# Projecting Q, K and V of a recurrent attention segment on four column groups of the TensorEngine, with V placed by DMA

## The chip, the cores and the metric

The kernel runs on one core of a Trainium2 chip. The metric is the device time of one launch in microseconds (us); smaller is better. Timed runs of a kernel and of the kernel before alternate on the same chip. The engines are named as in the profile: PE is TensorE (PEld its weight loads), DVE is VectorE, ACT is ScalarE, POOL is GpSimd, SP is SyncE, which here only issues DMAs.

## The reference, cut to what matters

The program is one training step (outputs and all gradients) of a block with a recurrent memory and a feed-forward layer, for 2048 tokens of 448 features. The tokens are cut into 64 segments of 32. Each segment is attended together with 8 memory rows, and the memory rows that come out are the input of the next segment. So 64 segments form a chain, forward, and another, backward.

```python
for s in range(n_seg):                        # 64 segments
    xs = x[:, s * seg_len:(s + 1) * seg_len, :]          # 32 rows of layernorm(x)
    h = jnp.concatenate([mem, xs], axis=1)               # 8 + 32 = 40 rows
    q = jnp.einsum('btd,dhe->bhte', h, Wq)               # 16 heads of 256
    k = jnp.einsum('btd,dhe->bhte', h, Wk)
    v = jnp.einsum('btd,dhe->bhte', h, Wv)
    scores = jnp.einsum('bhqe,bhke->bhqk', q, k) * scale
    p = _softmax(jnp.where(mask[None, None], scores, -1e9), axis=-1)
    o = jnp.einsum('bhqk,bhke->bhqe', p, v)
    o = jnp.einsum('bhte,hed->btd', o, Wo)
    mem = o[:, :M, :]                                    # 8 rows, to the next segment
    outs.append(o[:, M:, :])
# then h = x + outs, h2 = h + FFN(layernorm(h)); gradients of all of it by vjp
```

Everything but the memory rows is known from the start. Only `mem` is handed on, and it passes through every step above.

## The kernel before: the parts that matter

The kernel has four stages: the forward chain, the feed-forward stage, the backward chain, and a tail that computes the weight gradients.

In the forward chain, Q and K come out *feature-major* (features on the partitions): 32 blocks of 128 features, each with the 40 tokens as the moving operand. V comes out token-major on two column groups of 64.

```python
def wpass(W_sb, s, dst):                       # Q and K: 128 matmuls of 40 columns each
    ...
    for j in range(MC):                        # 32 blocks of 128 features
        for kc in range(KC):                   # 4
            nc.tensor.matmul(pss[b][:, jj * L:(jj + 1) * L], lhsT=W_sb[:, kc, c * P:(c + 1) * P],
                             rhs=hT_roll[:, kc, sl, :], ...)
# in the loop over segments, in the order in which they are written:
wpass(Wq_sb, s, qT)
wpass(Wk_sb, s, kT)
...                                            # scores, 32 short matmuls
for b in range(4):                             # V: 32 matmuls of 64 x 512
    for kc in range(KC):
        for g in range(2):
            nc.tensor.matmul(pV[b][64 * g:64 * g + 64, 0:512], lhsT=hT_flat[:, kc, sl * L:sl * L + 64],
                             rhs=Wv_sb[:, kc, n * 512:(n + 1) * 512], ...)
...                                            # softmax, evacuate V, transpose P
...                                            # P times V (16 matmuls); split off the 8 memory rows as o8
for j in range(MC):                            # memory rows times Wo
    nc.tensor.matmul(pO[32 * (j % 4):32 * (j % 4) + M, 0:D], lhsT=o8[:, j, :], rhs=Wo_sb[:, cj(j), :], ...)
...                                            # fp32 transposition of the sum of four groups -> hT_roll of s + 1
nc.gpsimd.dma_start(out=dr["QT"][s], in_=qT.rearrange("p c n -> p (c n)"))
nc.sync.dma_start(out=dr["KT"][s], in_=kT.rearrange("p c n -> p (c n)"))
```

The 32 x rows of four segments go through Wo together, as a full block of 128 rows, off the chain. The backward chain needs Q and K token-major, so it loads them with DMA transposes, and the tail reads whole tiles of attention rows from DRAM:

```python
def load_seg(s):                               # backward chain
    nc.sync.dma_start_transpose(out=vT..., in_=dr["VG"][s])
    nc.sync.dma_start_transpose(out=Q_sb, in_=dr["QT"][s])
    nc.sync.dma_start_transpose(out=K_sb, in_=dr["KT"][s])
...
src = dr["X_" + nm][t][:, hf * 2048:(hf + 1) * 2048]     # tail: one DMA, 128 partitions outermost
if nm == "o":
    nc.sync.dma_start(out=x_t, in_=src)
```

## Time and profile before

The kernel before took 3456.91 us (median of 3 runs, 3451.01 to 3477.07). The stages, read from the first and last instructions of each in the trace:

| stage of the kernel before | us |
|---|---|
| start to the first memory rows written for segment 1 | 82.5 |
| 62 more segments, 17.37 each on average | 1076.7 |
| end of the chain to the first feed-forward matmul | 84.2 |
| feed-forward | 322.7 |
| to the start of the backward chain | 44.8 |
| backward chain to the start of the tail | 1138.2 |
| tail | 712.6 |

The period of a segment is the time between two copies of the memory rows into the activations of the next segment (DVE, line 449).

One segment of the forward chain in the timeline of PE (columns: start, duration, engine, line, operation, operands, count; in brackets the idle time before it and what ended it):

```profile
604.24 6.55 PE L360 MATMUL psf<-arA,arW 128*128 128x40 bf16 x256 [0.28 <-DVE arA L449]
611.53 3.62 PE L399 MATMUL psf<-arW,arA 128*64 128x512 bf16 x30
615.16 0.38 PE L420 MATMUL psf<-ident,arB 128*40 128x40 bf16 x16
616.62 0.73 PE L428 MATMUL psf<-arB,arA 128*128 128x80 bf16 x16 [1.08 <-ACT arB L77]
617.42 1.69 PE L437 MATMUL po<-arW,arB 128*8 128x448 bf16 x32
```

Q and K (line 360) take 6.55 us, V (399) 3.62; the softmax runs under V; then P is transposed (420), P·V (428) waits 1.08 us for the evacuated P, and the memory rows go through Wo (437). Two stretches of the trace (window; length; busy time of each engine with its instruction count; clock; DMA share; GB/s), one in the forward chain and one in the backward chain:

```profile
300.00:600.00 300.00, 283.25 (x6902) 218.91 (x6899) 129.73 (x295) 96.38 (x211) 46.05 (x106) 0.99 0.45 141
1700.00:2200.00 500.00, 465.01 (x10749) 328.80 (x10753) 230.14 (x584) 187.33 (x485) 105.44 (x239) 0.98 0.78 166
```

PE is busy for 94% of the forward stretch. The DMA engines are busy for 45% there, and for 78% in the backward chain. What PE waited for in the forward chain from 80 to 1160 us (columns: what waited, what ended the wait; us in total, times, longest):

```profile
PE psf L428 <- ACT arB L77: 34.7, 32, 1.1
PE psf L446 <- DVE om L442: 9.0, 18, 0.6
```

There is little to wait for. So the forward chain is bound by PE's work.

### The profile page before, as it was taken

The numbers are of one execution on the slowest core, as the hardware profiler recorded it, in microseconds if no ns is written. First come the engines' busy times: TensorE is split into PE (matmuls) and PEld (weight loads), VectorE is DVE, ScalarE is ACT, GpSimd is POOL, SyncE is SP. The second block draws the span as 40 slices with busy tenths as digits, with TensorE's granted clock in tenths as the row PEclk, the third lists the DMA queues.
The fourth block names the chain that finished last, engine by engine and source line by source line (L and its number), as shares of the span: only waits on it lengthen the run. The fifth ranks groups of instructions, "written<-read, shape, count | busy, mean of one in ns | idle before, by whom it ended". The sixth has DMA issues, their size and how long they took to land.

```text
span 3461.7 us, 120955 instructions
## 1 busy us (share of the span) xinstructions
PE 3042.7 (88%) x55028; PEld 2056.9 (59%) x55038; DVE 1321.4 (38%) x2921; ACT 974.9 (28%) x2181; POOL 620.8 (18%) x1304
## 2 busy tenths in 40 slices
PE   3999999999999658892999999989999898999999
PEld 2777777777777446661666666666666544444444
DVE  4444444444444246771444444444444301111111
ACT  1333333333333223330333333333333202111100
POOL 3111111111111111111112211211221211111121
PEclk8999999999999879996999999999999999999999
DMA  7344633543534797799687878787887988888661
GB/s 264 132 130 133 174 127 130 162 146 127 156 130 147 134 210 182 178 212 239 139 164 167 174 161 165 166 160 163 172 167 162 275 241 185 174 176 179 160 247 38
DMA packets 997173, 583.91 MB, mean 169 GB/s; under 512 B 906100, under 2 KB 916420, under 8 KB 995060
## 3 DMA queue, kind: packets, MB, share of 16 engines
q1 hardware_dynamic: 926788, 340.27, 47.5%
q0 software_dynamic: 67568, 233.95, 19.8%
q8 instruction: 430, 7.05, 0.9%
q10 hardware_dynamic: 2304, 1.97, 0.2%
q14 instruction: 83, 0.68, 0.1%
HBM read 104.05 MB, written 250.19 MB: 102 GB/s over the span
## 4 chain that ended last, share of the span: by engine, by line
PE 61%; issue 13%; DMA 9%; DVE 8%; SPq 4%; ACT 2%; POOL 2%; ACTq 0%; DVEq 0%; POOLq 0%
PE psf L360 12%; PE po L756 8%; PE psf L399 6%; PE psf L713 5%; PE psf L691 4%; PE po L437 3%; PE fx L462 3%; PE fx L815 3%; PE psf L536 2%; PE psf L921 2%; PE psf L942 2%; PE psf L778 2%; DVE arA L75 2%; PE psf L446 2%; PE fx L602 2%
## 5 line engine op out<-in xcount | busy, mean ns | idle before, releaser
L77 ACT CAST arA<-psf 128x320 bf16<-128x320 f32 (+4 forms) x1139 | 487.9, 447 | 1595.2 <-PE psf L360 422.0
L75 DVE CAST arA<-psf 128x384 bf16<-128x384 f32 (+6 forms) x1029 | 492.5, 496 | 1075.9 <-PE psf L921 359.9
L360 PE MATMUL psf<-arA,arW 128*128 128x40 bf16 x16384 | 433.6, 181 | 62.0 <-POOL arA L345 35.8
L360 PEld LDWEIGHTS <-arW 128*128 128x128 bf16 x16384 | 432.2, 97 | 76.5 <-issue 57.3
L756 PE MATMUL po<-arW,arA 128*32 128x448 bf16 x6144 | 359.2, 365 | 40.5 <-DVE arA L75 21.0
L713 PE MATMUL psf<-arA,arW 128*128 128x40 bf16 x8192 | 219.2, 180 | 55.5 <-POOL arA L648 44.8
L921 PE MATMUL psf<-arW,arA 128*128 128x512 bf16 x990 | 250.7, 381 | 10.3 <-DMA arW<-X_k 5.3
L713 PEld LDWEIGHTS <-arW 128*128 128x128 bf16 x8192 | 214.9, 96 | 75.2 <-issue 74.8
L399 PE MATMUL psf<-arW,arA 128*64 128x512 bf16 x2048 | 259.5, 382 | 0.0
L756 PEld LDWEIGHTS <-arA 128*32 128x32 bf16 x6144 | 156.3, 98 | 160.7 <-issue 32.9
L536 PE MATMUL psf<-arA,arW 128*128 128x256 bf16 x1344 | 163.8, 283 | 94.4 <-DMA arA<-arA 68.7
L921 PEld LDWEIGHTS <-arA 128*128 128x128 bf16 x1440 | 135.2, 98 | 184.7 <-issue 39.2
L536 PEld LDWEIGHTS <-arW 128*128 128x128 bf16 x1344 | 136.3, 102 | 124.3 <-issue 100.4
L399 PEld LDWEIGHTS <-arA 128*64 128x64 bf16 x2048 | 147.3, 111 | 66.5 <-issue 0.2
L75 DVE CAST arB<-psf 40x320 bf16<-40x320 f32 x320 | 108.0, 337 | 98.1 <-PE psf L428 64.7
L77 ACT CAST arB<-psf 128x96 bf16<-128x96 f32 (+1 forms) x320 | 98.3, 307 | 103.5 <-DVE arB L75 51.0
L691 PEld LDWEIGHTS <-arW 128*128 128x128 bf16 x2048 | 88.4, 101 | 65.7 <-issue 62.1
L723 ACT COPY arA<-psf 128x1024 bf16<-128x1024 bf16 x128 | 123.3, 1015 | 4.7 <-PE psf L722 3.1
L462 PE MATMUL fx<-arW,arA 128*128 128x448 bf16 x512 | 124.5, 353 | 0.0
L437 PE MATMUL po<-arW,arB 128*8 128x448 bf16 x2048 | 110.7, 359 | 3.7
L691 PE MATMUL psf<-arB,arW 128*128 128x80 bf16 x2048 | 99.1, 203 | 16.7 <-DVE arB L740 7.7
L942 PE MATMUL psf<-arW 128*128 128x448 bf16 x450 | 95.4, 361 | 5.4 <-DMA arW<-X_o 5.3
(461 smaller groups left out, 3760.6 us busy)
## 6 DMA issues: line engine op xcount, KB each, us to landing
QT<-arA POOLq DMA_DIRECT2D x64, 512.0 KB, 4.0
KT<-arA SPq DMA_DIRECT2D x64, 512.0 KB, 3.5
VG<-arA SPq DMA_DIRECT2D x64, 512.0 KB, 3.1
X_o<-arA POOLq DMA_DIRECT2D x40, 512.0 KB, 4.5
X_v<-arA POOLq DMA_DIRECT2D x32, 512.0 KB, 6.2
X_k<-arA POOLq DMA_DIRECT2D x32, 512.0 KB, 4.2
X_q<-arA POOLq DMA_DIRECT2D x32, 512.0 KB, 4.2
arW<-X_o SPq DMA_DIRECT2D x30, 512.0 KB, 13.9
```

Source lines behind the costliest of these rows:

```text
L75: nc.vector.tensor_copy(out=out, in_=in_)
L77: nc.scalar.copy(out=out, in_=in_)
L360: nc.tensor.matmul(pss[b][:, jj * L:(jj + 1) * L], lhsT=W_sb[:, kc, c * P:(c + 1) * P], rhs=hT_roll[:, kc, sl, :], start=(kc == 0), stop=( ...
L399: nc.tensor.matmul(pV[b][64 * g:64 * g + 64, 0:512], lhsT=hT_flat[:, kc, sl * L:sl * L + 64], rhs=Wv_sb[:, kc, n * 512:(n + 1) * 512], sta ...
L437: nc.tensor.matmul(pO[32 * (j % 4):32 * (j % 4) + M, 0:D], lhsT=o8[:, j, :], rhs=Wo_sb[:, cj(j), :], start=(j < 4), stop=(j >= MC - 4), sk ...
L462: nc.tensor.matmul(px[:, 0:D], lhsT=xblk[:, j, :], rhs=Wo_sb[:, cj(j), :], start=(j == 0), stop=(j == MC - 1))
L536: nc.tensor.matmul(ps[:, f2 * 256:(f2 + 1) * 256], lhsT=Wt[:, kc, c * P:(c + 1) * P], rhs=xT[:, kc, :], start=(kc == 0), stop=(kc == KC - 1))
L691: nc.tensor.matmul(ps[b][:, i * 2 * L:(i + 1) * 2 * L], lhsT=lhs[:, cl, :], rhs=rhs_bd[:, cl // 2, :, :].rearrange("p g n -> p (g n)"), st ...
L713: nc.tensor.matmul(pss[b][:, jj * L:(jj + 1) * L], lhsT=WoT_sb[:, kc, c * P:(c + 1) * P], rhs=do_roll[:, kc, sl, :], start=(kc == 0), stop ...
L756: nc.tensor.matmul(pH[32 * (j % 4):32 * (j % 4) + 32, 0:D], lhsT=blk[nm][:, j, r * SEG:(r + 1) * SEG], rhs=WT[:, cj(j), :], start=(nm == " ...
L921: nc.tensor.matmul(pa[2 * kc + g][:, 0:w], lhsT=lhs_of(b)[:, kc * P:(kc + 1) * P], rhs=rhs_of(b, g), start=(b == 0), stop=(b == nblk - 1), ...
L942: nc.tensor.matmul(pa[i][:, 0:D], lhsT=lhs_of(b, i), rhs=rhs_of(b), start=(bi == 0), stop=(bi == len(nblk) - 1))
```

## The change

The intent is to take work off PE. A segment's 32 rows (24 of its own x rows and the 8 memory rows) fill one of four column groups of 32. The stationary operand is those 32 rows, the moving operand 512 columns of weights, and four groups run side by side. Q, K and V become six such passes, token-major. The remaining 8 x rows of each segment, which depend on nothing, are projected separately in batches of four segments (`rest`). Scores need Q and K feature-major, so 16 PE transposes are added. The four groups leave V in four partition ranges, while P·V needs it in two, so four small DMAs per segment move it (four more place the rows of `rest`). Heads are done in two halves so that the softmax of one half lies under the passes of the other. Q and K are stored token-major, so the backward chain loads them without DMA transposes. The output product now covers all 32 rows.

The core of the diff (cut; `...` marks the cuts):

```diff
+def col_pass(k, ps, W_sb, rows, b):
+    Wv = W_sb.rearrange("p c (g h d n) -> p c g h d n", g=2, h=8, d=2)
+    for kc in range(k.KC):
+        for q in range(4):
+            k.nc.tensor.matmul(ps[quad(q), 0:512], lhsT=rows(kc), rhs=Wv[:, kc, q % 2, 4 * b:4 * b + 4, q // 2, :], ...)
...
-            wpass(Wq_sb, s, qT)
-            wpass(Wk_sb, s, kT)
...
+            proj(Wk_sb, 0, Kst, "s")
+            proj(Wq_sb, 0, Qst, "v")
+            to_features(0)
+            pS0 = scores(0)
+            proj(Wv_sb, 0, Vst, "s")
+            proj(Wv_sb, 1, Vst, "s")
+            softmax(0, pS0)
+            proj(Wk_sb, 1, Kst, "s")
+            proj(Wq_sb, 1, Qst, "v")
+            to_features(1)
+            for q in range(4):
+                dc, g = divmod(q, 2)
+                nc.sync.dma_start(out=Vs[64 * g + M:64 * g + L, dc * 1024:(dc + 1) * 1024], in_=Vst[quad(q), :])
+            pS1 = scores(1)
+            transposed_p(0)
+            softmax(1, pS1)
+            values(0)
+            out_proj(0)
+            transposed_p(1)
+            values(1)
+            out_proj(1)
...
-        nc.sync.dma_start_transpose(out=Q_sb, in_=dr["QT"][s])
-        nc.sync.dma_start_transpose(out=K_sb, in_=dr["KT"][s])
+        for nm, X_sb in (("Q", Q_sb), ("K", K_sb)):     # ... four plain loads each, two full and two of the 8 rows
...
-            if nm == "o":
-                nc.sync.dma_start(out=x_t, in_=src)
+            elif nm == "o":
+                src = dr["Os"][4 * t:4 * t + 4].rearrange("r (d g i) c -> d g r i c", d=2, g=2)
+                for g in range(2):
+                    nc.sync.dma_start(out=x_t[:, g * 1024:(g + 1) * 1024], in_=src[hf, g])
...
-    for t0, t1 in ((0, 4), (4, NT), (NT + 1, NB), (NT, NT + 1)):
-        nc.gpsimd.dma_start(out=DCt[:, t0:t1], in_=dcs[:, t0:t1])
+    for g in range(NG):                                  # 4 + 16 small loads of gradient rows
+        nc.gpsimd.dma_start(out=DCt[:, NT + g], in_=dc8[g, :, 0:M])
+    for t0, t1 in ((NT // 2, NT), (0, NT // 2)):
+        for r in range(4):
+            nc.gpsimd.dma_start(out=DCt[32 * r:32 * r + 24, t0:t1], in_=dcx[r, M:SEG, t0:t1])
+            nc.gpsimd.dma_start(out=DCt[32 * r + 24:32 * r + 32, t0:t1], in_=dcm[r, :, t0:t1])
```

## The prediction

Written before anything of the changed kernel was built or run:

> What bounds the kernel now. The busy table by stretches puts the forward chain (64 dependent segments) at about 65 to 1180 us, the feed-forward stage to 1565, the backward chain to 2745, the tail to 3462. The timeline of TensorE in the forward chain repeats every 17.0 to 17.2 us (17.5 mean), over 90% busy: Q and K as 256 matmuls of 40 columns, 6.55 us (26 ns each); scores 0.85; V on two column groups 3.62; P transposed 0.38, then a wait of 1.08; P times V 0.73; memory rows times Wo 1.69; wait 0.50; fp32 transposition 1.27; wait 0.28. The blocks of the x rows times Wo (6.2 us per four segments) fill waits. So TensorE binds, with the softmax hidden under V.
>
> What changes. Q, K and V become six passes of 16 matmuls, 32 stationary columns by 512, on four column groups. The Trainium skill (TensorEngine Tiling (Array Packing), Performance Considerations) gives up to 4x for 32 columns and warns that evacuation isn't sped up. This trace agrees on the first: the backward row products (32 columns x 448, four groups) start 45 ns apart. Estimate from that: 52 ns x 96 = 5.1 us per segment, where Q, K and V took 10.2. Added: 16 transposes (1.1 us, as the 16 of the backward chain), the eight left-out x rows batched per four segments (estimate 6.2 us per tile, 1.6 per segment), two mask matmuls. The output product costs about as before (64 short matmuls, 1.7 us) but now covers 24 x rows, so most of the fill-in work goes. TensorE work falls from about 16.7 to 13.8 us per segment.
>
> But the dependent path doesn't fall by that. Estimate with durations of this trace: six passes plus first transposes and scores 6.1 us, then serially: Q evacuation 0.75 after the pass drains (0.3), transposes 0.5, their copy 0.7 to 0.9 (a 1024-wide bf16 copy took 0.69), scores 0.6, half softmax 2.1 (VectorE 160-wide ops about 0.33 each), P transposition and copy 0.7, values 0.4, copy 0.5, output 1.2, copy 0.45, fp32 transposition 1.27, copy 0.28: about 16.2 us with ideal order, near 16.9 with VectorE collisions (the batched rows' evacuations) and imperfect order. The chain turns from TensorE-bound to latency-bound; about half a microsecond to one is gained per segment, 30 to 60 us in all. V through DMA needs about 3 us from evacuation (stores land in 3.1) and has about 5, so should be hidden.
>
> Elsewhere: start +5 us (the batched rows need all three weights first); the feed-forward start waits for statistics written to and read from DRAM, +0 to +15 us beside a 62 us idle stretch already there, set by DMA transposes; backward loses two DMA transposes per segment (DMA share 0.78 falls), but TensorE binds there (93% busy), so 5 to 15 us; tail within 5 us.
>
> Predicted 3405 us, range 3310 to 3480. Chances: faster 0.32, same 0.53, slower 0.15.
>
> Right if: forward period 16 to 17.2 us with TensorE busy about 80% and waits before the second transposes, second scores and second P transposition; passes near 0.85 us; backward period unchanged within 0.3 us; DMA share lower in the backward chain.
>
> Wrong if: the order of instructions leaves the first half's waits unfilled (period 18 to 19.5), V's DMA arrives late behind DMA transposes on the same queue, the four groups don't overlap (passes over 1.2 us), the feed-forward start slips by a full DMA-transpose train (30 us); or, the other way, evacuations overlap better than I think and the period nears 15.

## More of the kernel before

The head of the profile's page: busy times, then the busy share in tenths in 40 slices of the span. PEclk is the granted TensorE clock in tenths of full speed.

```profile
span 3461.7 us, 120955 instructions
PE 3042.7 (88%) x55028; PEld 2056.9 (59%) x55038; DVE 1321.4 (38%) x2921; ACT 974.9 (28%) x2181; POOL 620.8 (18%) x1304
PE   3999999999999658892999999989999898999999
PEclk8999999999999879996999999999999999999999
```

PE is the busy engine in every stage, and its clock is nearly always full.

## The result

The changed kernel is correct and took 3759.17 us (median of 4 runs, 3733.73 to 3773.23) against 3466.99 us of the kernel before (4 runs, 3451.01 to 3485.98). The ratio is 1.082, with a 95% interval of 1.0755 to 1.0885. Here and below, a ratio is the record's own estimate from the fast runs of the same rounds, so not quite the ratio of the medians quoted. The prediction was wrong: the kernel is 8% slower.

The head of the page after:

```profile
span 3763.0 us, 108595 instructions
PE 3123.2 (83%) x47420; PEld 1874.6 (50%) x47430; DVE 1408.8 (37%) x3401; ACT 954.5 (25%) x2292; POOL 847.7 (23%) x1789
PE   3888888898888858876599999999997079989998
PEclk8888888898888878998799999999999589999999
```

PE executed 7,608 fewer matmuls and yet was busy for 80 us longer. PEclk tells why: it reads 8 instead of 9 in all but one of the slices of the forward chain. A second thing to see is the 7 and the 0 in the row of PE, slices 31 and 32, at the start of the tail. A ledger of the two profiled runs, by the stages of the table above (the period is now read at line 531):

| stage | before | after | difference |
|---|---|---|---|
| start to the first memory rows | 82.5 | 94.1 | +11.6 |
| 62 segments | 1076.7 | 1258.7 | +182.0 |
| period of one | 17.37 | 20.30 | +2.93 |
| end of the chain to feed-forward | 84.2 | 69.6 | −14.6 |
| feed-forward | 322.7 | 337.7 | +15.0 |
| to the backward chain | 44.8 | 28.6 | −16.2 |
| backward chain | 1138.2 | 1100.5 | −37.7 |
| tail | 712.6 | 873.8 | +161.2 |
| sum | 3461.7 | 3763.0 | +301.3 |

So two stages lose, the forward chain and the tail, and the backward chain gains. A stretch of each of the same two stages in the table by windows (the second 300 us later than before, since the stage starts later), and one at the start of the tail:

```profile
300.00:600.00 300.00, 263.58 (x4275) 146.45 (x4268) 131.27 (x365) 79.02 (x208) 93.77 (x208) 0.87 0.45 121
2000.00:2500.00 500.00, 478.51 (x11240) 340.79 (x11234) 243.85 (x621) 196.84 (x512) 113.39 (x258) 1.00 0.55 150
2890.00:3010.00 120.00, 6.02 (x34) 3.29 (x33) 4.05 (x10) 1.36 (x3) 13.74 (x22) 0.54 0.48 146
```

The forward clock fell from 0.99 to 0.87. The backward chain's DMA share fell from 0.78 to 0.55 and PE does more there. At the start of the tail PE is nearly idle for 120 us.

The list of PE's waits in the forward chain, 80 to 1160 us:

```profile
PE psf L488 <- DMA arA<-arA: 48.5, 53, 2.6
PE psf L488 <- issue: 23.0, 18, 3.1
PE po L500 <- DVE arA L75: 18.8, 57, 0.4
PE psf L527 <- ACT om L524: 17.6, 33, 0.5
```

Line 488 is P·V. It now waits for a DMA from SBUF to SBUF: the DMAs that place V. A part of the same wait is put under "issue". Counting every idle time of PE just before P·V, it is 1.75 us per segment; in the kernel before, such waits for V did not exist. One segment at full clock shows how the wait arises; first PE, then the queue on SP:

```profile
1315.08 2.76 PE L286 MATMUL psf<-arW,arA 128*32 128x512 bf16 x45
1317.77 0.40 PE L444 MATMUL psf<-ident,arA 128*128 128x128 bf16 x4
1319.67 0.23 PE L488 MATMUL psf<-arB,arA 128*128 128x80 bf16 x2 [0.65 <-DMA arA<-arA]
1319.84 0.38 PE L455 MATMUL psf<-arA 128*40 128x40 bf16 x16
1322.22 0.38 PE L488 MATMUL psf<-arB,arA 128*128 128x80 bf16 x6 [2.00 <-DMA arA<-arA]
```

```profile
1316.81 2.44 SPq L515 DMA_DIRECT2D arA<-arA  x4
```

The passes themselves run as planned: 45 matmuls in 2.76 us. V's last evacuation ends at 1316.78 us (ACT, 0.57 us from 1316.21). The four DMAs take 2.44 us to be issued (2.44 is also the median of the 64 segments), and P·V with V's last part starts at 1322.22, that is 5.44 us after the evacuation. PE ran out of work twice, for 0.65 and 2.00 us.

The second loss is seen where the next segment begins after such a wait:

```profile
610.72 0.56 PE L488 MATMUL psf<-arB,arA 128*128 128x80 bf16 x6 [3.10 <-issue]
611.59 1.90 PE L500 MATMUL po<-arW,arA 128*32 128x256 bf16 x32 [0.32 <-DVE arA L75]
617.61 1.91 PE L527 MATMUL psf<-selq,om 128*128 128x32 f32 x8 [0.53 <-ACT om L524]
619.80 3.60 PE L286 MATMUL psf<-arW,arA 128*32 128x512 bf16 x32 [0.28 <-DVE arA L531]
```

The output product (500) takes 1.90 us, the fp32 transposition (527) 1.91, the first 32 matmuls of the passes (286) 3.60. At full clock the same three take 1.05, 1.08 and 1.91 us (shown below under vf_ot_sp_fill and oldv_fill). The clock records show windows of 3.413 us, each with a clock of 1.0 or 0.5. In the changed kernel, 86 of the 307 windows that begin from 150 to 1200 us were at half clock; in the kernel before, 13 of 308. Counted over the 62 segments, that is 6.15 us of each segment and 0.54.

At the start of the tail, the queue on SP, before and after:

```profile
2746.41 35.24 SPq L884 DMA_DIRECT2D arW<-X_o  x20
```

```profile
2904.44 89.49 SPq L1005 DMA_DIRECT2D arW<-Os  x25
```

and what PE waited for in the first part of the tail after (2885 to 3200 us):

```profile
PE fx L1070 <- DMA arW<-Or: 114.4, 2, 113.7
```

```profile
3009.14 0.55 PE L1070 MATMUL fx<-arW 128*128 128x448 bf16 x1 [113.67 <-DMA arW<-Or]
```

The tail reads the attention rows in blocks of 128 rows by 2048 columns, in two halves of the columns. The loads (`Os`) are issued at 3.6 us apiece for half a block, where the kernel before issued a whole block every 1.8 us (its longest wait for one was 1.9 us). PE waits 113.7 us once, for a later load (`Or`) that stands behind them in the queue. The trace shows one thing more. That load is the first one of the second half. In the order of PE's matmuls, two that belong to the second half (they write `fx` alone) stand after the first four blocks of the first half, and the other blocks come after them. When the two were done, the next eight blocks of the first half ran without a wait. So the wait has two causes, slow loads and this order. Of the kernels below, oldv, fill, vfirst, vf_ot, vf_ot_sp, vf_ot_sp_fill and oldv_fill have the same order; the kernel before, tail16, best and best_fill do not.

### The profile page after: what moved, and what is told of

It reads as the page before. It is cut to its first block, busy times and chain, and to the rows that moved or that the text cites. A ratio compares the mean times of both kernels' runs of the same rounds, so it can differ in the third digit from the quotient of the medians.

```text
span 3763.0 us, 108595 instructions
## 1 busy us (share of the span) xinstructions
PE 3123.2 (83%) x47420; PEld 1874.6 (50%) x47430; DVE 1408.8 (37%) x3401; ACT 954.5 (25%) x2292; POOL 847.7 (23%) x1789
## 4 chain that ended last, share of the span: by engine, by line
PE 50%; issue 17%; DMA 15%; DVE 8%; SPq 5%; ACT 3%; POOL 2%; ACTq 0%; POOLq 0%; DVEq 0%
PE psf L286 9%; PE po L874 6%; DMA arA<-arA 5%; PE po L500 4%; PE psf L831 4%; PE psf L809 3%; PE psf L648 3%; DVE arA L75 3%; PE psf L527 3%; PE fx L933 2%; PE fx L286 2%; PE psf L1049 2%; SPq L515 2%; DMA arA<-arW 2%; PE psf L444 2%
## 5 line engine op out<-in xcount | busy, mean ns | idle before, releaser
L75 DVE CAST arA<-psf 128x512 bf16<-128x512 f32 (+4 forms) x965 | 451.7, 487 | 1121.1 <-PE psf L1049 367.9
L77 ACT CAST arA<-psf 128x512 bf16<-128x512 f32 (+6 forms) x1011 | 414.8, 424 | 1614.6 <-PE psf L286 402.6
L286 PE MATMUL psf<-arW,arA 128*32 128x512 bf16 x6144 | 472.2, 432 | 48.2 <-POOL arA L389 36.3
L286 PEld LDWEIGHTS <-arA 128*32 128x32 bf16 x7680 | 206.5, 103 | 264.7 <-issue 69.6
L831 PE MATMUL psf<-arA,arW 128*128 128x40 bf16 x8192 | 218.5, 180 | 35.0 <-DMA arW<-KR 28.7
L831 PEld LDWEIGHTS <-arW 128*128 128x128 bf16 x8192 | 214.6, 96 | 54.4 <-issue 53.9
L1049 PEld LDWEIGHTS <-arA 128*128 128x128 bf16 x1440 | 137.0, 99 | 188.3 <-issue 45.2
L874 PEld LDWEIGHTS <-arA 128*32 128x32 bf16 x6144 | 154.0, 97 | 153.7 <-issue 39.0
L500 PE MATMUL po<-arW,arA 128*32 128x192 bf16 (+1 forms) x4096 | 174.8, 307 | 24.4 <-DVE arA L75 24.2
L648 PEld LDWEIGHTS <-arW 128*128 128x128 bf16 x1344 | 136.8, 102 | 112.1 <-issue 83.5
L77 ACT CAST arB<-psf 40x160 bf16<-40x160 f32 (+3 forms) x448 | 120.5, 269 | 191.7 <-PE psf L476 160.0
L1070 PEld LDWEIGHTS <-arW 128*128 128x128 bf16 x606 | 59.9, 99 | 187.8 <-DMA arW<-Or 115.3
L500 PEld LDWEIGHTS <-arA 128*32 128x32 bf16 x4096 | 126.9, 111 | 52.2 <-DVE arA L75 45.3
L286 PE MATMUL fx<-arW,arA 128*32 128x512 bf16 x1536 | 137.5, 385 | 0.9 <-DVE arA L75 0.8
L488 PEld LDWEIGHTS <-arA 128*128 128x128 bf16 x1024 | 56.8, 108 | 160.4 <-issue 76.2
L444 PEld LDWEIGHTS <-arA 128*128 128x128 bf16 x1024 | 62.8, 102 | 131.9 <-ACT arA L77 55.5
L444 PE MATMUL psf<-ident,arA 128*128 128x128 bf16 x1024 | 108.2, 233 | 22.7 <-ACT arA L77 16.2
```

Source lines behind the costliest of these rows:

```text
L75: nc.vector.tensor_copy(out=out, in_=in_)
L77: nc.scalar.copy(out=out, in_=in_)
L286: k.nc.tensor.matmul(ps[quad(q), 0:512], lhsT=rows(kc), rhs=Wv[:, kc, q % 2, 4 * b:4 * b + 4, q // 2, :], start=(kc == 0), stop=(kc == k.K ...
L444: nc.tensor.transpose(ph[:, (i * HB + h) * P:(i * HB + h + 1) * P], st[:, (HB * b + h) * P:(HB * b + h + 1) * P], ident[:, :])
L488: nc.tensor.matmul(po[:, i * 2 * L:(i + 1) * 2 * L], lhsT=Vs[:, dc * 1024 + h * P:dc * 1024 + (h + 1) * P], rhs=PT_bd[:, h, :, :].rearrang ...
L500: nc.tensor.matmul(pO[quad(2 * dh + jh), 0:w], lhsT=o32[:, j, :], rhs=Wo_sb[:, cj(j), 256 * dh:256 * dh + w], start=(j < 2), stop=(j >= MC ...
```

## The experiments

From these traces I took three theories. **V**: the V placement is late, and PE's wait for it costs the forward chain. **C**: these waits push PE's activity so low that its clock is halved, and that costs about as much again. **T**: the tail loses because the new loads have an outermost dimension of four. The rivals: the dependent path is simply longer than I had estimated, so that taking the waits away gives little; and the tail loses to the many small gradient loads. A third, the order of PE's matmuls seen above, was given no run of its own. This table gathers the forward period, the half-clock time and the idle time just before P·V, each per segment, from the profiled run of each:

| kernel | median us | ratio (95%) | period | half clock | before P·V |
|---|---|---|---|---|---|
| before | 3466.99 | 1 | 17.37 | 0.54 | – |
| changed | 3759.17 | 1.082 (1.0755–1.0885) | 20.30 | 6.15 | 1.75 |
| tail16 | 3674.44 | 1.0591 (1.0546–1.0637) | 20.41 | 6.38 | 1.75 |
| oldv (wrong result) | 3636.34 | 1.0484 (1.0415–1.0554) | 18.03 | 3.04 | 0.28 |
| fill | 3711.95 | 1.0708 (1.0671–1.0745) | 19.64 | 1.87 | 0.80 |
| vfirst | 3663.65 | 1.0572 (1.0531–1.0612) | 18.99 | 4.41 | 0.67 |
| vf_ot | 3595.05 | 1.0372 (1.0319–1.0425) | 19.28 | 4.57 | 0.90 |
| vf_ot_sp | 3583.03 | 1.0333 (1.029–1.0375) | 19.28 | 4.80 | 0.85 |
| vf_ot_sp_fill | 3553.85 | 1.0238 (1.0213–1.0263) | 18.45 | 0.88 | 0.68 |
| oldv_fill (wrong result) | 3561.65 | 1.0319 (1.0275–1.0362) | 17.43 | 0.22 | 0.06 |
| best | 3619.16 | 1.0499 (1.0465–1.0533) | 19.48 | 4.96 | 0.84 |
| best_fill | 3589.42 | 1.0397 (1.0358–1.0435) | 18.80 | 1.43 | 1.12 |
| before_plain (wrong result) | 3452.7 | 0.9938 (0.9907–0.9969) | 17.49 | 0.66 | – |
| before_tok | 3477.47 | 1.0015 (0.9974–1.0055) | 17.93 | 0.81 | – |

And the tail by part: the part that reads the attention rows (o), and the part of v, k and q. The gate and up part took 90.1 us in every kernel; the last 50 us or so are left out.

| kernel | o part | v, k, q part |
|---|---|---|
| before | 133.7 | 438.2 |
| changed | 267.5 | 461.7 |
| tail16 | 200.9 | 436.6 |
| vf_ot | 174.1 | 463.4 |
| vf_ot_sp_fill | 173.4 | 466.8 |
| best | 138.6 | 480.0 |
| oldv_fill | 266.9 | 437.5 |

### tail16: the tail's loads with 32 partitions outermost

```diff
-                for g in range(2):
-                    nc.sync.dma_start(out=x_t[:, g * 1024:(g + 1) * 1024], in_=src[hf, g])
+                for g in range(2):
+                    for r in range(4):
+                        nc.sync.dma_start(out=x_t[32 * r:32 * r + 32, g * 1024:(g + 1) * 1024], in_=src[hf, g, r])
```

> Only the loads of the stored output rows at the start of the tail change: each (4 x 32 rows of 2 KB) is cut into four of 32 rows. Theory A: a load whose outermost dimension is 4 runs on four of the sixteen DMA engines (between 2960 and 2980 us of the kernel after, the 2 KB packets of that queue took 84 us in 20 us, so about four at a time), 8 MB through four engines take over 100 us, and TensorE stands still for 114 us. Then the tail (first TensorE work to the end) falls from 874 us to 700 to 750 and the whole from 3760 to 3600-3640. Rival: the stand-still comes from the new order of the blocks or from late gradient rows; then at least 70 us of it stay and the whole stays above 3690.

It took 3674.44 us, in between the two expectations. The o part fell by 66.6 us, from 267.5 to 200.9, against the 133.7 of the kernel before. PE's waits in the tail's first part, for comparison with the single wait of 113.7 us:

```profile
PE psf L1071 <- DMA arW<-Os: 33.6, 8, 16.6
```

So cutting the loads gave back half of the tail's loss in the o part. But PE's order changed with it: the two matmuls of the second half no longer stand ahead, so how much of the 66.6 us is the loads' shape alone isn't separated. And the wait of 16.6 us ended 22.9 us after the tail's first matmul, when the last of the small gradient loads for that block had just landed (22.6 us). The Trainium skill ("DMA: Bandwidth & Descriptors", the section on why a DMA increments its semaphore by 16) says that a DMA is spread over the largest number of engines, at most 16, that divides the slowest dimension of both sides. For a leading dimension of 4 that means four engines, and the changed kernel's trace agrees: between 2960 and 2980 us, 956 packets of 2 KB took 83.3 us of engine time in 20 us, about 4.2 at once. The rest of the loss is followed by vf_ot and best below.

### oldv: P·V reads the other segment's V buffer, so nothing waits for the placement

```diff
-                            nc.tensor.matmul(po[...], lhsT=Vs[:, dc * 1024 + h * P:dc * 1024 + (h + 1) * P], ...)
+                            nc.tensor.matmul(po[...], lhsT=V_b[(s + 1) % 2][:, dc * 1024 + h * P:dc * 1024 + (h + 1) * P], ...)
```

The result is wrong (relative error 1.40); the work is the same.

> Wrong result on purpose: P times V reads the V buffer of the segment before, so that it never waits for the DMA that places V; everything else is issued as in the kernel after. Theory B: V arrives late (four issues of about 0.6 us each after the last evacuation, then 2.9 us to land), TensorE idles about 2 us per segment for it, and this idling also halves the granted clock for the next passes. Then the forward period falls from 20.3 us to 16.5-17.5 and the whole by 180-240 us, to 3520-3580, with the first two passes of a segment near 1.8 us instead of 3.6. If V's wait costs only its own idle time: period 18 to 18.8, the whole near 3640. Rival C: the chain of evacuations is what costs; period above 19.5.

The period fell by 2.27 us, to 18.03, although only 1.47 us of idle time before P·V went away (1.75 to 0.28). The half-clock time halved, from 6.15 to 3.04 us per segment. In the 24 segments that had no half-clock time at all, the period was 16.98 us. So V is shown, and the remainder beyond the wait fits C. My range for both losses together, 16.5 to 17.5 us, was missed: 18.03 us and 3636 us lie where I had put V's own idle time alone, because much of the half clock stayed.

### fill: dummy matmuls while V is on its way

```diff
             transposed_p(0)
             softmax(1, pS1)
+            pfill = k.fx1()
+            for i in range(12):
+                nc.tensor.matmul(pfill[:, 0:512], lhsT=ident[:, :], rhs=Wq_sb[:, 0, 512 * (i % 8):512 * (i % 8) + 512], start=True, stop=True)
             values(0)
```

Twelve matmuls whose result nobody reads, in a PSUM tile of their own.

> Twelve matmuls of 128 x 512 whose result nobody reads are put ahead of the first P times V of each segment, where TensorE waits for V: about 2.6 us of work per segment at full clock, the result stays right. Theory B with the clock part: the granted clock in the forward chain rises from 0.85 to above 0.95, the first two passes take about 1.8 us instead of 3.6, and the period falls by 1.5 to 3 us although work was added: the whole 3570-3670. If idling does not set the clock (low clock from the 32-column passes themselves or from elsewhere): period equal or up to 1 us longer, 3760-3830.

More work for PE made the kernel faster: a ratio of 1.0708 (1.0671 to 1.0745) where the changed kernel has 1.082 (1.0755 to 1.0885). The half-clock time fell from 6.15 to 1.87 us per segment and the period from 20.30 to 19.64. The stretch from 300 to 600 us:

```profile
300.00:600.00 300.00, 283.67 (x4429) 151.49 (x4426) 132.15 (x366) 78.67 (x207) 92.76 (x203) 0.94 0.45 121
```

With the clock at 0.94 instead of 0.87 the rest of the segment went faster, at the price of the fillers themselves. I had expected more (a period shorter by 1.5 to 3 us, a whole of 3570 to 3670), but the rival, an equal or longer period, is out. So C is a cause of its own. It is the smaller one in this form, since the wait for V stays in the path.

### vfirst: V projected first

```diff
+            proj(Wv_sb, 0, Vst, "s")
+            proj(Wv_sb, 1, Vst, "s")
+            for q in range(4):
+                dc, g = divmod(q, 2)
+                nc.sync.dma_start(out=Vs[64 * g + M:64 * g + L, ...], in_=Vst[quad(q), :])
             proj(Wk_sb, 0, Kst, "s")
             ...
             pS0 = scores(0)
-            proj(Wv_sb, 0, Vst, "s")
-            proj(Wv_sb, 1, Vst, "s")
```

> The two V passes and the four DMAs that place V move ahead of the first K pass; result right. Theory B: V has landed before P times V is due, so period 16.5 to 17.5 us, granted clock above 0.95, the whole 3520-3580. If the wait for V is only replaced by waits for the K and Q evacuations (rival C): period above 19.

The result is right. In the program the V passes now stand two passes earlier and the DMAs four; PE's P·V begins long after they were issued:

```profile
608.12 2.44 SPq L507 DMA_DIRECT2D arA<-arA  x4
615.78 0.54 PE L488 MATMUL psf<-arB,arA 128*128 128x80 bf16 x8
```

The period fell by 1.31 us, to 18.99. In PE's list of waits from 80 to 1160 us, P·V waited for the DMA twice, where it had waited 53 times for 48.5 us:

```profile
PE psf L488 <- DMA arA<-arA: 3.6, 2, 2.1
```

Still, my range (16.5 to 17.5 us, the whole 3520 to 3580) was missed, and the period is next to the rival's 19. The half-clock time was still 4.41 us per segment, beside new or longer waits (for evacuated Q and K, P and O, none over 0.8 us), and the segments without any half clock took 17.67 us, more than the 17.37 of the kernel before. This is the first sign that the order which hides V makes the rest of the path longer.

### vf_ot: V first, and attention rows stored as whole tiles

```diff
-        nc.gpsimd.dma_start(out=dr["Os"][s], in_=stg)
+        nc.gpsimd.dma_start(out=dr["Ot"][t].rearrange("(r i) (q c) -> r q i c", r=4, q=4)[r], in_=stg)
...
-                src = dr["Os"][4 * t:4 * t + 4].rearrange("r (d g i) c -> d g r i c", d=2, g=2)
-                for g in range(2):
-                    nc.sync.dma_start(out=x_t[:, g * 1024:(g + 1) * 1024], in_=src[hf, g])
+                nc.sync.dma_start(out=x_t, in_=dr["Ot"][t][:, hf * 2048:(hf + 1) * 2048])
```

(plus the edit of vfirst). The store now does the gathering, and the tail loads whole tiles as the kernel before did.

> V first, and the output rows stored tile by tile so that the tail loads each block with one DMA of 128 rows of 4 KB, as the kernel before does; result right. Theory A (the four-row outer dimension, and after that the many small DMAs, starve the tail): the tail falls from 865-874 us to 705-730, the whole from 3664 (V first alone) to 3500-3530. Rival (order of the blocks and the 20 small gradient loads cost the rest): tail above 750, the whole above 3545.

By my numbers the rival won: the tail took 779.2 us (above 750) and the whole 3595 us (above 3545). The o part is 174.1 us: 27 us better than tail16, which issued eight small DMAs per block, and still 40 us above the kernel before. Its one long wait is again for the first `Or` load of the second half:

```profile
PE fx L1068 <- DMA arW<-Or: 30.0, 1, 30.0
```

The forward period rose a little, from 18.99 to 19.28 us. The edit touched only the store there; why it costs 0.3 us per segment was not looked into.

### vf_ot_sp: the batched rows spread over three segments

```diff
-            if t + 1 < NT:
-                rest(t + 1)
+        if r < 3 and t + 1 < NT:
+            rest(t + 1, (r,))          # K's part, Q's part, V's part
```

> As the run before it, and the batched eight rows are emitted in three parts over three segments rather than all in one. If the clock falls in segments that have no such fill-in work: the forward period goes from 19.0 to 17.8-18.7 us, the whole 3440-3500. If the order on TensorE comes out much the same, or fill-in work isn't what keeps the clock: no change within 20 us of the run before it.

Nothing in the forward chain: 19.28 us in both, and the times differ by less than the intervals (1.0372 and 1.0333). When the batched rows are projected is not what costs.

### vf_ot_sp_fill: the same, with dummy matmuls in the short waits

```diff
+            def fill(ps, n):
+                for i in range(n):
+                    nc.tensor.matmul(ps[:, 0:512], lhsT=ident[:, :], rhs=Wq_sb[:, 0, 512 * i:512 * i + 512], start=True, stop=True, ...)
...                                    # into PSUM tiles that the next product overwrites:
+                    fill(pPT, 4 if b == 1 and g == 0 else 0)      # before the second transposition of P
+                    fill(po, 2 if b == 1 and x == 0 else 0)       # before the second P·V
+            fill(pm, 2)                                           # before the fp32 transposition
```

> As the run before it, with eight matmuls of 128 x 512 per segment that nobody reads (1.7 us at full clock), four ahead of the second P transposition, two ahead of the second P times V, two ahead of the last transposition; result right. Theory of the clock (a 3.4 us stretch in which TensorE is busy less than half to two thirds of the time is followed by one at half clock, and only a stretch that is almost full ends it): granted clock above 0.95 in the forward chain, period 16.8 to 17.8 us, the whole 3390-3450, although work was added. If the added work simply adds: period 19.5 to 20.5, the whole above 3530.

The result is right. Eight useless matmuls per segment took 29 us off the kernel. The half-clock time fell from 4.80 to 0.88 us per segment and the period from 19.28 to 18.45 us (median 17.88). By my numbers the theory was half right: the period lies between the two expectations (16.8 to 17.8, and 19.5 to 20.5 if the added work simply adds), but the whole above 3530, where I had put the rival. Two of the three operations shown at half clock above are here at full clock, though part of a segment's work is now dummy:

```profile
713.68 1.05 PE L509 MATMUL po<-arW,arA 128*32 128x256 bf16 x32
715.42 1.08 PE L537 MATMUL psf<-selq,om 128*128 128x32 f32 x8
```

This is the fastest correct descendant of the change, and it is still 2.4% slower than the kernel before. 49 segments had no half-clock time; they took 17.96 us.

### before_plain: the kernel before without the two DMA transposes per segment in the backward chain

```diff
-        nc.sync.dma_start_transpose(out=Q_sb, in_=dr["QT"][s])
-        nc.sync.dma_start_transpose(out=K_sb, in_=dr["KT"][s])
+        nc.sync.dma_start(out=Q_sb.rearrange("p a b -> p (a b)"), in_=dr["QT"][s])
+        nc.sync.dma_start(out=K_sb.rearrange("p a b -> p (a b)"), in_=dr["KT"][s])
```

Q and K are then in the wrong layout (relative error 1.22); the work is the same.

> The kernel before, with wrong results on purpose: in the backward chain Q and K are loaded as they lie by plain DMAs instead of by DMA transposes; nothing else changes. If the two transposes were what the backward chain gained from (1138 us before, 1100 after): the backward chain takes 1095-1115 us and the whole falls by 20 to 45 us, to 3415-3440. If its gain came from elsewhere (another order of instructions): less than 12 us.

The backward chain's instructions spanned 1104.3 us instead of 1141.0, a gain of 36.7. In the changed kernel they spanned 1103.2. The stretch from 1700 to 2200 us, beside the 465.01 us and the DMA share of 0.78 above:

```profile
1700.00:2200.00 500.00, 474.56 (x11083) 337.28 (x11082) 236.86 (x601) 192.81 (x499) 109.51 (x249) 0.98 0.59 170
```

So the backward gain of the change is the two transposes, and nothing else is needed to explain it. Its size is less sure: in before_again, the same kernel once more, the backward chain spanned 1131.7 us, 9.3 less than in the first profile, which makes the gain 27.4. The whole kernel gained 0.6%.

### oldv_fill: neither the wait for V nor the half clock

The edits of oldv, of vf_ot_sp, and dummies (3, 1 and 1). V stays in its original place in the order. Wrong, as oldv.

> Wrong result on purpose: P times V reads the V buffer of the segment before (no wait for V), the batched rows are spread over three segments, and five 128 x 512 matmuls that nobody reads (1.1 us) fill the waits near the end of a segment. In the first run without the wait, the 24 segments that met no half-clock stretch took 16.98 us. If V's wait and the half clock are all that made the chain slower than its estimate of 16.9: period 16.8-17.5 us with the clock above 0.96, the forward first-to-last distance 1045-1085 us (1259 in the kernel after). If something else is missing from the account: above 18.

This run measures the dependent path of the change with both losses taken away: a period of 17.43 us (median 17.27), with 0.22 us of half clock and 0.06 us before P·V per segment. The start of a segment in its timeline, which gives the full-clock durations of the transposition and of the first 32 matmuls, and the busy tenths of PE and its clock from the head of its page:

```profile
605.40 1.08 PE L537 MATMUL psf<-selq,om 128*128 128x32 f32 x8 [0.32 <-ACT om L533]
606.76 1.91 PE L286 MATMUL psf<-arW,arA 128*32 128x512 bf16 x32 [0.28 <-DVE arA L541]
```

```profile
PE   3999999999999378873999999999995179999999
PEclk9999999999999689996999999999998589999999
```

In the forward chain (slices 2 to 13) both rows read 9 throughout, as in the kernel before, whose period was 17.37 us. So taking V and C away gives back 2.87 of the 2.93 us per segment. In this form the change then gains nothing in the forward chain. The five dummies are part of it, though: of PE's 16.2 us of busy time per segment here, 15.2 are the kernel's own work (ends of matmuls are modelled), against 16.3 in the kernel before. In oldv, which has no dummies, the 24 segments free of half clock took 16.98 us, where the kernel before takes 17.1 in segments of the same places. So without dummies too, no more than about 0.2 us is in sight.

### best and best_fill: the gradient rows gathered earlier

```diff
+    dh3 = dr["DHb"][0:S, :].rearrange("(s r) d -> s r d", r=SEG)          # start of the backward chain
+    nc.gpsimd.dma_start(out=dr["DC"][0:S, :].rearrange("(s r) d -> s r d", r=SEG)[:, 0:SEG - M, :], in_=dh3[:, M:SEG, :])
+    nc.gpsimd.dma_start(out=dr["DC"][S:, :].rearrange("(s m) d -> s m d", m=M), in_=dh3[:, 0:M, :])
...
-    ...                                     # the 20 small loads of the diff above
+    dcs = dr["DC"].rearrange("(t p) d -> p t d", p=P)[:, :, 0:D]
+    for t0, t1 in ((NT, NB), (NT // 2, NT), (4, NT // 2), (0, 4)):
+        nc.gpsimd.dma_start(out=DCt[:, t0:t1], in_=dcs[:, t0:t1])
...
-        nc.sync.dma_start(out=dr["VG"][s], in_=Vs)
+        nc.gpsimd.dma_start(out=dr["VG"][s], in_=Vs)
```

(best is vf_ot_sp with these; best_fill has dummies 3, 1 and 1 besides.) These were meant as the best version that the reasons so far pointed to.

> Right result: V first, tile-wise output rows, spread rows, the store of V moved to the GpSimd queue so that the SyncE queue no longer stands behind V's landing, and the gradient rows gathered in DRAM ahead of time so that four DMAs instead of twenty load them. Tail: if the twenty small gradient loads cause the 30 us stand-still left at its start, the tail falls from 770 to 710-735 us; if it is the order of the blocks, it stays above 750. Forward: period 18.0 to 19.2 us. The whole 3490-3540.

> The run before it with five matmuls per segment that nobody reads, in the waits near the end of a segment; result right. Forward period 17.2-17.9 us at a clock above 0.96, tail as in the run before it, the whole 3420-3470, so within 1% of the kernel before. Above 3500 if the account of the forward chain is wrong.

The names turned out wrong: 3619.16 and 3589.42 us, ratios of 1.0499 and 1.0397, where vf_ot_sp and vf_ot_sp_fill stood at 1.0333 and 1.0238. The expectations fell with them: best's tail took 759.4 us, above the 750 that I had put for the order of the blocks as the cause (the v, k and q part rose, see below), best_fill's forward period was 18.80 us instead of 17.2 to 17.9, and its whole lies above the 3500 that I had put for a wrong account of the forward chain. That a correct kernel can be rid of both losses at once is therefore not shown. The o part did fall, from 174 to 138.6 us, next to the 133.7 of the kernel before. Its long wait is now a shorter one, for gradient rows:

```profile
PE psf L1066 <- DMA arW<-DC: 13.6, 1, 13.6
```

The 20 small loads had their part in the 35 us: in vf_ot_sp the last of those that the fifth block needs landed 35.7 us after the tail's first matmul, just when PE's wait ended; in best it landed after 19.7 us. But PE's order is another one in best as well, and the two aren't separated. And the gathering copies took it back: the backward chain, at whose start they run, spanned 1128.2 and 1140.8 us where the other descendants have 1097 to 1107. The v, k and q part rose to 480.0 and 472.6 as well. And the forward chain did not profit from another queue for the store of V (19.48 against 19.28).

### before_tok: the one part of the change that gained, alone

```diff
-        nc.gpsimd.dma_start(out=dr["QT"][s], in_=qT.rearrange("p c n -> p (c n)"))
-        nc.sync.dma_start(out=dr["KT"][s], in_=kT.rearrange("p c n -> p (c n)"))
+        for nm, xT in (("QT", qT), ("KT", kT)):
+            ot = stg()
+            nc.sync.dma_start_transpose(out=ot.rearrange("p (a b) -> p a b", b=P), in_=xT.rearrange("p c n -> p (c n)"))
+            nc.gpsimd.dma_start(out=dr[nm][s], in_=ot)
```

(and plain loads in the backward chain as in before_plain). Here the transposes are moved from the backward chain, where the DMA share was 0.78, to the forward chain, where it was 0.45. The result is right.

> The kernel before, with one idea of the change kept and all else undone: its forward chain transposes Q and K by DMA from SBUF to SBUF and stores them token-major, and its backward chain loads them with plain DMAs. The result should be right. Theory (the DMA engines have room in the forward chain, where their share was 0.44, and none in the backward chain, where it was 0.78): the backward chain falls from 1141 to about 1104 us as in the run before_plain, the forward period stays at 17.3 to 17.6 us, and the whole is 10 to 30 us shorter, a ratio of 0.991 to 0.997. Rival (the transposes cost the same wherever they stand, since they block the queue that also carries the x loads): the forward period goes above 17.8 us, and the ratio is 1.00 or more.

My theory fell. The backward chain did shrink, to 1108.5 us, but the forward period rose from 17.37 to 17.93 us, and the ratio is 1.0015 (0.9974 to 1.0055): the same time. The two stretches:

```profile
300.00:600.00 300.00, 275.94 (x6726) 216.08 (x6726) 122.37 (x278) 90.32 (x198) 52.88 (x121) 0.98 0.86 197
1700.00:2200.00 500.00, 468.88 (x11003) 334.54 (x11007) 234.78 (x597) 192.12 (x498) 104.11 (x238) 0.99 0.57 165
```

The DMA share of the forward chain doubled, from 0.45 to 0.86. The added wait in the forward chain is put under "issue" in front of the first Q matmul (21.5 us in 24 waits, 6.9 in 12 before), so its releaser isn't shown. That the transposes block the queue, as the rival had it, remains argued; that they cost about the same in either chain is measured (forward +35 us in all; backward −32.5, or −23.2 against before_again).

### after_again and before_again: how much of the ledger is chance

The two kernels once more, unchanged.

> The changed kernel once more, not a letter different. What it tells: the feed-forward stage took 337.7 us in the profile of the changed kernel and 322.7 us in that of the kernel before, and the v, k and q part of the tail 461.7 against 438.2 us, with the same code in both. Theory (these two stages vary from run to run of one kernel, so that 39 us of the difference of the two profiles are chance): at least one of the two here differs by over 5 us from what the first profile showed, and the other stages (the forward period, the part of the tail with the o rows) agree within 1%. Rival (the change sets them, by the moment at which the stage starts or by where its tensors lie): both agree with the first profile within 5 us.

> The kernel before once more, not a letter different, for the same question. Theory (they vary from run to run): the feed-forward stage or the v, k and q part of the tail differs by over 5 us from the 322.7 and 438.2 us of its first profile. Rival (set by the kernel): both within 5 us.

One run each (state unknown): 3775.61 and 3455.75 us. The forward period repeats to 0.02 us (20.29 and 17.38), the o part to 2.4 us (265.1 and 134.0), and the feed-forward stage to 3 us (340.7 and 324.0). So the 15 us of the feed-forward stage are not chance, as far as one repeat of each can tell. Over all kernels it ran from 316.0 us (vf_ot) to 342.9 (tail16), with the same code; before_plain, which differs from the kernel before only in later loads, took 330.7. What sets it was not found. The backward chain repeats in the changed kernel (1103.2 us both times), but not in the kernel before (1141.0 and 1131.7). The v, k and q part moved by 12 us in the changed kernel (461.7 to 474.0) and by 4 in the kernel before (438.2 to 442.6), so its difference of 23.5 us between the two profiles may in part be chance.

## Why the prediction was wrong, point by point

**The bound before and the passes: right; the work saved: too high.** PE bound the forward chain, and the column groups worked: 45 matmuls in 2.76 us, 61 ns each with the last one's drain (54 ns from one start to the next), next to the estimated 52. The Trainium skill ("TensorEngine Tiling (Array Packing)", Performance Considerations), which the prediction named, gives a tiling factor of four for 32 columns, and says that evacuation is not sped up. The traces agree with the first as far as they go: 512-column matmuls started 108 ns apart on V's two groups of 64 columns before, and 54 ns apart on the four groups. They don't contradict the second: DVE, which does much of the evacuation, was busy for 7.5 us per segment before and 8.9 after (from the stretches of 300 to 600 us). But PE's own work fell by 1.1 us per segment (16.3 to 15.2, oldv_fill), not by the 2.9 of "about 16.7 to 13.8". The second output product, for one, takes 2 × 1.05 us, where 1.7 had been counted.

**"V through DMA needs about 3 us from evacuation (stores land in 3.1) and has about 5, so should be hidden": wrong, and the first step that failed.** Two numbers were off, each by about 2 us. V needed 5.44 us in the segment shown, since the four DMAs are issued one after the other in 2.44 us; the prediction had counted one landing and no issuing. And it had less time than thought: PE stood idle for 2.65 us of those 5.44, which leaves 2.8 us covered. The risk itself was named in the prediction ("V's DMA arrives late"), though for another reason, DMA transposes ahead of it in the queue; in 62 of the 64 segments the issue begins 0.03 us after an evacuation, so nothing stood ahead of it. oldv shows the size: without the wait the period falls by 2.27 us.

**The clock: missing from the estimate.** All durations in the sum were taken at the full clock of the kernel before, and the prediction itself expected PE to be busy for only about 80%. It did not ask what the clock does then. It was at half for 6.15 us of each segment. fill and vf_ot_sp_fill show that this is a cause and not only a symptom: dummy matmuls alone made the kernel faster. With both taken away (oldv_fill), the period is 17.43 us.

**"about 16.2 us with ideal order, near 16.9 with VectorE collisions": nearly right, but with almost no gain in it.** The measured counterparts are 17.43 us on average with dummies (oldv_fill) and 16.98 us in the 24 chosen segments of oldv. The kernel before took 17.37 us on average and 17.1 in the same places. The estimated gain of "30 to 60 us in all" in the forward chain was then near zero even in the best case measured, since the change replaced a segment bound by PE by a chain of dependent steps about as long. In the correct kernels that put V first, the segments without half clock took 17.67 (vfirst) to 17.96 us (vf_ot_sp_fill).

**"tail within 5 us": wrong by 156.** It was 161.2. The prediction gives no reason for its 5 us; the shape of the new loads doesn't appear in it. Of the 134 us in the o part, some 67 went with the outermost dimension of four (tail16), 27 with the many small DMAs (vf_ot against tail16), and 35 with the small gradient loads (best against vf_ot_sp). In all three steps PE's order changed as well, so the three sizes are not those of the loads alone. The first cause was to be read from the diff: the access pattern is in it.

**Backward, "so 5 to 15 us": right cause, too small.** It was 37.7; before_plain alone gives 36.7 (27.4 against before_again). The prediction held that PE binds there (93% busy). PE was busy for 465.01 us of 500 before and for 478.51 after, so part of the idle 7% was the transposes' after all.

**Start +5, feed-forward start 0 to +15.** The start cost 11.6 us more. The start of the feed-forward stage came 14.6 us *earlier* relative to the end of the chain, and the backward chain's start 16.2 us earlier. These were not tested.

The sum of the measured terms: +182.0 forward, +161.2 tail, −37.7 backward, −4.2 in the rest of the ledger, together +301.3 us.

**What stays open.** Why the feed-forward stage has another length in each kernel with the same code (+15.0 us here). What moves the v, k and q part between 437 and 480 us. And whether a correct form of the change can reach 17.43 us: it would need V earlier without pushing Q and K later.

## What to carry to other kernels

When a change turns an engine-bound loop into a chain of dependent steps, add up the chain at its real durations, with the issue time of every DMA in it, before crediting the work saved; here the saved PE work was worth next to nothing, because the chain was about as long as the segment had been. Idle time on TensorE inside a short loop can cost twice, as it did here: once as the wait, and once through the clock, which slowed the dependent steps that followed. And when a change stores data in a new layout, follow every later reader of it: the loads with an outermost dimension of four went with the largest single loss in the tail here, 67 us. Where PE waits for a load, look also at whether it needed that load yet.

## What the Trainium skill lacked or had wrong

- "TensorE: Matmul & The Clock Gate" (Part 1 and the table of rules) ties the half clock to one idle window of 3413 ns, and its rule is to have no idle gaps over about 3 us; a section on a second failure mode says that frequent small gaps can do it too, without saying how many. The trace agrees on the window (3.413 us) and on the two levels (1.0 and 0.5). But here shorter gaps were enough: of the 28 windows at full clock in the changed kernel (150 to 1200 us) that were followed by half clock, none had an idle gap over 3.1 us, and the median of their longest gaps was 1.38 us; in vfirst it was 0.78 us in 23 windows. In the changed kernel the busy share of the window goes with it: of the windows under 50% busy (by the modelled ends of matmuls) 22 of 22 were followed by half clock, of those between 50 and 70%, 6 of 14, of those over 70%, 0 of 185. It isn't the whole rule: in the kernel before, 8 windows that were 76 to 90% busy were followed by a single one at half clock, and what set these off is not known.
- The same page says that one busy window brings the clock back, without saying how busy. In the changed kernel half-clock windows that were 75 to 90% busy were followed by another one in 48 of 48 cases, and those over 95% in 0 of 25.
- The same page's remedies are loop order and padding; none fits a chain of dependent steps. One that worked here: eight dummy 128x512 matmuls per segment in short waits cut the half-clock time from 4.80 to 0.88 us per segment, and 29 us off the kernel (vf_ot_sp against vf_ot_sp_fill).
- "DMA: Bandwidth & Descriptors" gives a fixed cost of about 2 us per DMA on the GpSimd path, and I found no issue time there for a small DMA on the SyncE queue of this chip. Here four DMAs of 32 partitions x 1024 bf16, SBUF to SBUF, took 2.44 us to issue, 0.6 us each, and the last had landed 2.97 us later (1319.25 to 1322.22 us).
- The same page (Latency and other measured facts) gives 261 GB/s for a DMA transpose with a non-contiguous middle dimension in one kernel. In before_tok, two SBUF to SBUF transposes of 128x2048 bf16 per segment raised the DMA share from 0.45 to 0.86. By an estimate from these shares and the periods (0.86 × 17.93 − 0.45 × 17.37 = 7.6 us for two), one of 524,288 bytes took all sixteen engines for 3.8 us, about 138 GB/s.
